# A long convolution done as two half-length transforms on a matmul array: 72 array fills in place of 96

## The chip, the core and the metric

The kernel runs on one core of a Trainium2 chip. A core has a matmul array (TensorE, PE in the profile), three engines for elementwise work (VectorE or DVE, ScalarE or ACT, GpSimd or POOL), a queue engine (SyncE or SP) that here issues nearly all transfers, and 16 DMA engines that carry them out. The metric is the time of one execution on the device in microseconds (us).

## What is computed

With S = 2048 positions and D = 512 channels:

```python
k_shift = sum(k_pad[:, t:t + S, :] * shift_k[:, ks - 1 - t] for t in range(4))   # 4 taps, causal
kv = k_shift * v
y = irfft(rfft(pad(kv)) * rfft(pad(ssm_k)))[:S]      # causal convolution of length S, one per channel
a = q * (y + kv * ssm_D)
b = relu(q @ w1) @ w2                                 # D -> 1792 -> D
g = sigmoid((q * gate_w).sum(-1))
out = g * a + (1 - g) * b
```

## The kernel before

**Two independent lines of work share the engines.** The one is the MLP b. Its inputs are split into a high and a low part, so that each product takes three matmuls of 128x512 (lines 310 to 312 for the first layer, 340 to 342 for the second). It runs in two eras of seven hidden blocks each, over four chunks of 512 positions. ACT writes the high part of the hidden block (`hh`, line 323), DVE the low part (`hl`, line 326); lines 257 and 260 split the loaded inputs and weights.

**The other is the convolution,** a transform of complex length 2048 in two steps, 64 times 32, such that the real part of the product's inverse is the causal convolution. It has three stages, with a round through DRAM between them:

- *First stage* (`stage1`, eight chunks, each of two of the 16 columns into which the positions of a partition are laid): DVE makes kv (lines 439 to 455), then for the filter (`s1h`) and for kv (`s1x`) the array applies a 64-point transform. One matmul takes 64 rows to 128 (real and imaginary part of 64 frequencies), so two of them, side by side on the array, fill it once. ACT copies each result to an `ev` tile and SP stores it in the DRAM tensor `sa` (line 395): 64 stores.
- *Middle stage* (`conv_mid`, eight sets g of 256 complex frequencies): SP loads four `r` tiles from `sa` (line 473, eight transfers a set) and the constants `cc`; the array does the 32-point transforms with 64x32 tiles, two fills for the filter (`f_h`) and two for kv (`f_x`, line 498); the filter's spectrum is copied to `ha` by DVE and ACT in turn (line 521); DVE makes the complex product, eight multiplications (line 533) and four sums (line 540) of 128x512 into `p`; the array applies the inverse 32-point transform in two fills of 32x64 tiles (`iv`, line 554); `bv` copies (lines 565 and 567) and four stores to `sb` (line 562) end the set. The inverse of set g-1 is issued in front of the transforms of set g.
- *End* (`conv_end`, four groups of four columns n): SP loads a `br` tile from `sb` for each n (line 599), the array applies the inverse 64-point transform, one fill each (`cy`, line 619), and DVE combines the result with q and the gate (lines 606 to 633) and with the MLP (line 580).

The second stage starts when all stores to `sa` have landed (`phase(2)`), the third when all stores to `sb` have (`phase(3)`). The four `r` tiles are as many as one set takes: the next set's loads wait until the fills of this set have read them.

**A planner writes the order of each engine's instructions** before the program is built (`Plan.order`). It plays the work through with a fixed cost for each operation and a room for each kind of buffer, and lets the convolution's fills go ahead of the MLP's matmuls as soon as their inputs are there by that reckoning. On the chip each engine then follows its list in order and waits where an input is late; this goes for SP too, whose transfers are issued one after another.

The transfers that matter here name their two sides in this way, the tile's side being 128 partitions of 512 values:

```python
nc.sync.dma_start(sa["hx".index(t), :, 16 * half + R * c + r], T["ev" + t, c, half, r])                                            # 395
nc.sync.dma_start(T[k("r", t, u)][:, i * D:(i + 1) * D], sa["hx".index(t), 4 * j:4 * j + 4].rearrange("k n d -> (k n) d"))      # 473
nc.sync.dma_start(sb[m:m + 4].rearrange("k n d -> (k n) d"), T[k("bv", j)])                                                      # 562
nc.sync.dma_start(rows(tile_of(k("br"), "br", 2 * D)), sb[:, n::16])                                                             # 599
```

Of the kernel before, what the change touches and what calls it, by code (L numbers as in the profile page):

```python
# [14 lines left out]
P = 128  # L15
# [25 lines left out]
def _constants():  # L41

    n1, k1 = np.arange(64)[:, None], np.arange(64)[None]
    w = _w((4 * k1 + 1) * 32 * n1)
    s1 = np.stack([w.real, w.imag], -1).reshape(64, 128)
    s1 = np.concatenate([s1, s1], 0)

    fw = np.zeros((2, 2, 32, NJ, 2, 32))  # L50
    iv = np.zeros((4, 32, 8, 2, 2, 2, 32))
    n2, k2 = np.arange(32)[:, None], np.arange(32)[None]
    for j in range(NJ):
        for b in range(2):
            k1 = 2 * j + b
            c = _w((4 * k1 + 1 + 256 * k2) * n2)
# [4 lines left out]
            c = np.conj(c.T)  # L61
            iv[j % 4, :, j // 4, 0, b, 0] = c.real
            iv[j % 4, :, j // 4, 1, b, 0] = -c.imag
            iv[j % 4, :, j // 4, 0, b, 1] = c.imag
            iv[j % 4, :, j // 4, 1, b, 1] = c.real
    cc = np.concatenate([fw.reshape(P, 8, 2 * P), iv.reshape(P, 8, 2 * P)], 2)


    c = np.conj(_w((4 * np.arange(64)[:, None] + 1) * 32 * np.arange(64)[None])) / S
    ib = np.stack([c.real, -c.imag], 1).reshape(P, 64)  # L70
    return s1, cc, ib
# [139 lines left out]
def build(tc, wf, xp, qn, kn, vn, hn, dn, sh, gw, w1, w2, cs1, ccc, cib, out):  # L211
# [13 lines left out]
    room = {"raw": RAW, "x": 4, "cv": 6, "m": 2, "hh": HB, "o": OB, "in": IN, "cc": 2, "acc": ACC, "tmp": TMP, "ev": EV, "r": RB,  # L225
# [150 lines left out]
    def stage1(c, rank, parts):  # L376

        ops = []
        deps = [s1ld] + [after for _, _, after, _ in parts]
        for t, key, after, give in parts:  # L380
            for r in range(R):
                def go(t=t, key=key, r=r):
                    z = slice(r * D, (r + 1) * D)
                    for half in range(2):
                        at = slice(64 * half, 64 * half + 64)
                        mm(bank(("s1" + t, c, half, r)), T["s1t",][at, :], T[key][at, z], start=True, stop=True)  # L386
# [12 lines left out]
        plan.chain(ops)  # L399
# [64 lines left out]
    def conv_load(g, gate):  # L464
# [12 lines left out]
        cc = add("SP", ISSUE, rank - 0.5, lambda: nc.sync.dma_start(tile_of(k("cc"), "cc", 4 * P), ccc[:, g]),  # L477
# [3 lines left out]
    def conv_mid(g, gate):  # L481
# [19 lines left out]
        last = list(ys.get(g - 1, {}).values())  # L501
# [10 lines left out]
        if g and IV_FIRST:  # L512
            put_iv(g - 1, ivp())
        fh = []
        ha = {}
        for o in range(2):
            f = link(TILES, lambda o=o: rounds("h", o), deps, ["cv"] * 2 + ["ha"] * 2, ["r"] * 2 if o else ())
            for b in range(2):
                cp = (nc.vector.tensor_copy if b == 0 else nc.scalar.copy)
                ha[o, b] = add("ACT" if b else "DVE", act_time(D, True) if b else dve_time(D), (0, rank),  # L520
                               lambda o=o, b=b, cp=cp: cp(tile_of(k("ha", o, b), "ha"), T[k("f", "h", o, b)]), [f], (), ["cv"], fifo=["ha"])
        if g and not IV_FIRST:
            put_iv(g - 1, ivp())
# [247 lines left out]
```

## Time and profile before

| what | value |
|---|---|
| median of 3 runs | 411.96 us (409.59 to 412.96) |
| the profiled execution | 410.51 us, of which 408.7 us are the span of the profile |
| busy: PE, DVE, ACT, POOL | 401.8, 274.2, 128.2, 1.4 us |
| PE clock granted | 0.999 of full speed |
| DMA | 90.94 MB, 222 GB/s over the span |

The span goes from the first instruction to the last. Busy times are those of single engines and overlap. A DMA share is the mean over the 16 DMA engines. In the tables of groups each row gives the line, the engine and the operation, the tile written and the tiles read, the count, the busy time and the mean duration of one; in the chain of work that ended last each row gives start, duration, engine, tile and line.

### The profile page before, as it was taken

To read this page: it belongs to the slowest core of one execution; us is meant where nothing else is said; L and a number is where in the kernel's file an instruction comes from. 1 tells how busy PE (TensorE), PEld (TensorE's weight loads), DVE (VectorE), ACT (ScalarE), POOL (GpSimd) and SP (SyncE) were. 2 spreads that over 40 slices of the span, in tenths; PEclk is the share of its full clock that TensorE was granted. 3 is DMA by queue.
4 is the path that set the end of the run, shared out by engine and by line. 5 is a ranking of instruction groups with operands and counts; after the bars stand their busy time and mean duration, and the time that the engine had idled before them with its cause. 6 is when DMAs were issued, how large, how long until landed. Compare 5 with 4: busy or idle time off the path is not lost.

```text
span 408.7 us, 6184 instructions
## 1 busy us (share of the span) xinstructions
PE 401.8 (98%) x2317; PEld 283.5 (69%) x2317; DVE 274.2 (67%) x420; ACT 128.2 (31%) x241; POOL 1.4 (0%) x6
## 2 busy tenths in 40 slices
PE   7999999999999999999999999999999999999996
PEld 6888667768667677667485857658478766765884
DVE  5699999745999302958785964968952577667511
ACT  6542552641554443421522320232411312002100
POOL 0000000000000000000000000000000000000000
PEclk9999999999999999999999999999999999999999
DMA  8986892994797784739684764837609684974011
GB/s 294 332 289 182 303 350 109 324 322 176 262 332 240 272 294 169 267 125 321 225 275 135 252 219 169 293 125 251 208 17 287 215 272 145 334 245 163 2 51 51
DMA packets 45487, 90.94 MB, mean 222 GB/s; under 512 B 4849, under 2 KB 5105, under 8 KB 45330
## 3 DMA queue, kind: packets, MB, share of 16 engines
q1 hardware_dynamic: 45394, 90.46, 64.8%
q8 instruction: 18, 0.29, 0.3%
q0 software_dynamic: 64, 0.10, 0.1%
q14 instruction: 11, 0.09, 0.1%
HBM read 61.18 MB, written 29.36 MB: 222 GB/s over the span
## 4 chain that ended last, share of the span: by engine, by line
PE 94%; DMA 3%; DVE 2%; ACT 0%; issue 0%; DVEq 0%; ACTq 0%
PE m L340 13%; PE m L341 12%; PE m L342 12%; PE m L310 11%; PE m L311 11%; PE m L312 11%; PE s1h L386 4%; PE f_h L498 4%; PE f_x L498 3%; PE s1x L386 3%; PE iv L554 3%; PE cy L619 3%; PE m L296 3%; DMA q<-qn 2%; DMA raw<-w 1%; DMA raw<-xp 1%
## 5 line engine op out<-in xcount | busy, mean ns | idle before, releaser
L340 PE MATMUL m<-w1h_h,hh 128*128 128x512 f32 x224 | 88.5, 395 | 0.0
L341 PE MATMUL m<-w1l_l,hh 128*128 128x512 f32 x224 | 87.4, 390 | 0.0
L342 PE MATMUL m<-w1h_h,hl 128*128 128x512 f32 x224 | 87.2, 389 | 0.0
L326 DVE SCALAR_TENSOR_TENSOR hl<-m,hh 128x512 fp32r<-128x512 f32 x56 | 38.3, 689 | 49.0 <-ACT hh L323 48.8
L323 ACT ACTIVATE hh<-m 128x512 fp32r<-128x512 f32 x56 | 33.3, 602 | 101.9 <-PE m L312 98.1
L310 PE MATMUL m<-xh_h,w0h_h 128*128 128x512 f32 x160 | 63.4, 396 | 0.4 <-DVE gs L611 0.4
L311 PE MATMUL m<-xl_l,w0h_h 128*128 128x512 f32 x160 | 62.4, 390 | 0.0
L312 PE MATMUL m<-xh_h,w0l_l 128*128 128x512 f32 x160 | 62.3, 389 | 0.0
L340 PEld LDWEIGHTS m<-w1h_h,hh 128*128 128x128 f32 x224 | 42.0, 188 | 17.3 <-issue 8.8
L342 PEld LDWEIGHTS m<-w1h_h,hl 128*128 128x128 f32 x224 | 42.0, 188 | 9.0
L341 PEld LDWEIGHTS m<-w1l_l,hh 128*128 128x128 f32 x224 | 42.1, 188 | 8.4
L310 PEld LDWEIGHTS m<-xh_h,w0h_h 128*128 128x128 f32 x160 | 30.0, 188 | 13.4 <-issue 5.7
L312 PEld LDWEIGHTS m<-xh_h,w0l_l 128*128 128x128 f32 x160 | 30.1, 188 | 6.4
L311 PEld LDWEIGHTS m<-xl_l,w0h_h 128*128 128x128 f32 x160 | 30.0, 188 | 5.9
L445 DVE TENSOR_TENSOR acc<-acc,tmp 128x1024 f32<-128x1024 f32 x24 | 29.3, 1223 | 0.6
L442 DVE TENSOR_TENSOR tmp<-in,sht_sht 128x512 f32<-128x512 f32 x32 | 21.3, 686 | 8.5 <-DMA in<-kn 8.3
L567 DVE COPY bv<-iv 128x512 f32<-128x512 f32 x16 | 10.3, 686 | 20.2 <-PE iv L554 20.2
L392 ACT COPY ev<-s1h 128x512 f32<-128x512 f32 x32 | 16.4, 599 | 19.7 <-PE s1h L386 17.7
L565 ACT COPY bv<-iv 128x512 f32<-128x512 f32 x16 | 8.6, 589 | 42.9 <-PE iv L554 36.0
L349 ACT COPY y<-m 128x512 f32<-128x512 f32 x16 | 9.4, 589 | 40.0 <-PE m L342 39.9
L533 DVE TENSOR_TENSOR p<-f_x,ha 128x512 f32<-128x512 f32 x32 | 19.9, 684 | 1.2 <-PE f_x L498 1.2
L533 DVE TENSOR_TENSOR ha<-f_x,ha 128x512 f32<-128x512 f32 x32 | 20.3, 681 | 0.0
(61 smaller groups left out, 449.4 us busy)
## 6 DMA issues: line engine op xcount, KB each, us to landing
sa<-ev SPq DMA_DIRECT2D x64, 256.0 KB, 4.2
r_h<-sa SPq DMA_DIRECT2D x32, 256.0 KB, 4.5
r_x<-sa SPq DMA_DIRECT2D x32, 256.0 KB, 5.2
sb<-bv SPq DMA_DIRECT2D x32, 256.0 KB, 3.6
br<-sb SPq DMA_DIRECT2D x16, 512.0 KB, 6.3
raw<-xp SPq DMA_DIRECT2D x28, 256.0 KB, 3.8
raw<-w SPq DMA_DIRECT2D x24, 256.0 KB, 4.3
in<-kn SPq DMA_DIRECT2D x10, 512.0 KB, 5.4
```

The lines of the kernel that those rows point to most:

```text
L310: mm(ps, part("h", f, k), T["x", "h", xe, c, k], start=k == 0, stop=False)
L311: mm(ps, part("h", f, k), T["x", "l", xe, c, k], start=False, stop=False)
L312: mm(ps, part("l", f, k), T["x", "h", xe, c, k], start=False, stop=k == 3)
L323: nc.scalar.activation(tile_of(("hh", era, c, f), "hh", dt=F32R, p=mp, bufs=HB), T["m1", era, c, f], AF.Relu)
L326: nc.vector.scalar_tensor_tensor(tile_of(("hl", era, c, f), "hl", dt=F32R, p=mp, bufs=HB), T["m1", era, c, f], 0.0, T["hh", era, c, f].bit ...
L340: mm(ps, T["hh", era, c, f][:, z], T["w", "h", 1, f], start=f == fs[0], stop=False)
L341: mm(ps, T["hh", era, c, f][:, z], T["w", "l", 1, f], start=False, stop=False)
L342: mm(ps, T["hl", era, c, f][:, z], T["w", "h", 1, f], start=False, stop=f == fs[-1])
L386: mm(bank(("s1" + t, c, half, r)), T["s1t",][at, :], T[key][at, z], start=True, stop=True)
L445: nc.vector.tensor_tensor(T["acc", c], T["acc", c], T[dst], op=OP.add)
L498: mm(ps[b][32 * j:32 * j + 32, :], T[k("cc")][at, 64 * j + 32 * o:64 * j + 32 * o + 32], T[k("r", t, j // 2)][at, (j % 2) * D:(j % 2 + 1) ...
L533: tt(src if o else tile_of(k("p", i, b), "p"), T[k("f", "x", o, b)], src, op=OP.mult)
```

## The change

The convolution is cut into halves of 1024 positions, filter and kv each. Both halves of both are transformed with complex length 1024 (32 times 32); the first half of the result is the product of the first halves, the second half comes from three products (first half by first half, turned by a quarter, and the two mixed ones), so three complex products take the place of one of twice the size.

- First stage: 32x64 tiles, eight to a fill, so one fill for each of filter and kv in a chunk where there were two. The two are no longer chained to one another. An `ev` tile now holds 64 rows for each of two positions.
- Middle stage: the fills are as many as before. The filter's spectrum goes into one `ha` tile of four planes, copied by ACT alone. DVE makes the products in five instructions, one over four planes and four over two, with the spectrum of kv read once per plane. GpSimd makes all sums, nine instructions over ten planes. The inverse of set g-2 (not g-1) is issued in front of set g.
- End: 64x32 tiles, one fill for two columns; a `br` tile holds two columns and is loaded by four transfers of 256 KB.
- `sa`, `sb` keep their shapes, with the 128 rows now (half, frequency, real or imaginary). The transfers to and from them take their DRAM side as 2 blocks of 64 rows. The rooms change with the tile sizes.

```diff
--- before.py
+++ after.py
-    n1, k1 = np.arange(64)[:, None], np.arange(64)[None]
-    w = _w((4 * k1 + 1) * 32 * n1)
-    s1 = np.stack([w.real, w.imag], -1).reshape(64, 128)
...
+    n1, k1 = np.arange(32)[:, None], np.arange(32)[None]
+    w = _w((4 * k1 + 1) * 64 * n1)
+    s1 = np.tile(np.stack([w.real, w.imag], -1).reshape(32, 64), (4, 1))
...
+    cc = np.concatenate([fw.reshape(P, 8, 2 * P), iv.reshape(P, 8, P)], 2)
...
+    ib = np.stack([c.real, -c.imag], 1).reshape(64, 32)
+    return s1, cc, np.tile(ib, (2, 1))
...
-    room = {"raw": RAW, "x": 4, "cv": 6, "m": 2, "hh": HB, "o": OB, "in": IN, "cc": 2, "acc": ACC, "tmp": TMP, "ev": EV, "r": RB,
...
-        ops = []
-        deps = [s1ld] + [after for _, _, after, _ in parts]
         for t, key, after, give in parts:
-            for r in range(R):
-                def go(t=t, key=key, r=r):
-                    z = slice(r * D, (r + 1) * D)
-                    for half in range(2):
-                        at = slice(64 * half, 64 * half + 64)
-                        mm(bank(("s1" + t, c, half, r)), T["s1t",][at, :], T[key][at, z], start=True, stop=True)
-
-                m = add("PE", TILES, (0, rank), go, deps if not ops else [ops[-1]], ["cv"] * 2, give if r == R - 1 else (), tiles=True)
-                ops.append(m)
-                for half in range(2):
-                    def out_(t=t, r=r, half=half):
-                        nc.scalar.copy(tile_of(("ev" + t, c, half, r), "ev"), T["s1" + t, c, half, r])
-
-                    def put(t=t, r=r, half=half):
-                        nc.sync.dma_start(sa["hx".index(t), :, 16 * half + R * c + r], T["ev" + t, c, half, r])
-
-                    v = add("ACT", act_time(D, True), (0, *rank), out_, [m], ["ev"], ["cv"])
-                    stores.append(add("SP", ISSUE, (-5000, *rank), put, [v], (), ["ev"], dma=ROW))
-        plan.chain(ops)
+            def go(t=t, key=key):
+                for a in range(4):
+                    ps = bank(("s1" + t, c, a))
+                    at = slice(32 * a, 32 * a + 32)
+                    for r in range(R):
+                        mm(ps[64 * r:64 * r + 64, :], T["s1t",][at, :], T[key][at, r * D:(r + 1) * D], start=True, stop=True)
+
+            m = add("PE", TILES, (0, rank), go, [s1ld, after], ["cv"] * 4, give, tiles=True)
+            for a in range(4):
+                def out_(t=t, a=a):
+                    nc.scalar.copy(tile_of(("ev" + t, c, a), "ev"), T["s1" + t, c, a])
+
+                def put(t=t, a=a):
+                    n = 16 * (a // 2) + R * c
+                    nc.sync.dma_start(sa["hx".index(t), 64 * (a % 2):64 * (a % 2) + 64, n:n + R].rearrange("m r d -> r m d"), T["ev" + t, c, a])
+
+                v = add("ACT", act_time(D, True), (0, *rank), out_, [m], ["ev"], ["cv"])
+                stores.append(add("SP", ISSUE, (-5000, *rank), put, [v], (), ["ev"], dma=ROW))
...
-                    nc.sync.dma_start(T[k("r", t, u)][:, i * D:(i + 1) * D], sa["hx".index(t), 4 * j:4 * j + 4].rearrange("k n d -> (k n) d"))
+                    src = sa["hx".index(t)].rearrange("(b m) n d -> b m n d", b=2)[:, 2 * j:2 * j + 2]
+                    nc.sync.dma_start(T[k("r", t, u)][:, i * D:(i + 1) * D], src.rearrange("b m n d -> b (m n) d"))
...
-        cc = add("SP", ISSUE, rank - 0.5, lambda: nc.sync.dma_start(tile_of(k("cc"), "cc", 4 * P), ccc[:, g]),
...
-        last = list(ys.get(g - 1, {}).values())
+        old = g - BEHIND
+        last = ys.get(old, [])
         if g < NJ // 4:
             h, x, cc = conv_load(g, gate)
             deps = h + x + [cc] + last
         else:
             deps = last
-        ivp = lambda: link(2 * TILES, lambda: inverse(g - 1), deps, ["cv"] * 4, ["p"] * 4 + ["cc"])
-        if g == NJ // 4:
-            put_iv(g - 1, ivp())
+        if old >= 0:
+            put_iv(old, link(2 * TILES, lambda: inverse(old), deps, ["cv"] * 4, ["p", "cc"]))
+        if g >= NJ // 4:
             plan.chain(chain)
...
+        planes = lambda z, u, n=2: T[k(z)][:, u * D:(u + n) * D].rearrange("p (r d) -> p r d", d=D)
+        ha = []
         for o in range(2):
-            f = link(TILES, lambda o=o: rounds("h", o), deps, ["cv"] * 2 + ["ha"] * 2, ["r"] * 2 if o else ())
+            f = link(TILES, lambda o=o: rounds("h", o), deps, ["cv"] * 2 + ([] if o else ["ha"]), ["r"] * 2 if o else ())
             for b in range(2):
-                cp = (nc.vector.tensor_copy if b == 0 else nc.scalar.copy)
-                ha[o, b] = add("ACT" if b else "DVE", act_time(D, True) if b else dve_time(D), (0, rank),
-                               lambda o=o, b=b, cp=cp: cp(tile_of(k("ha", o, b), "ha"), T[k("f", "h", o, b)]), [f], (), ["cv"], fifo=["ha"])
-        if g and not IV_FIRST:
-            put_iv(g - 1, ivp())
-        d = dve_time(D)
-        prev, y = {}, {}
-        for o in range(2):
-            fx = link(TILES, lambda o=o: rounds("x", o), deps, ["cv"] * 2 + ([] if o else ["p"] * 4), ["r"] * 2 if o else ())
-            for b in range(2):
-                for i in range(2):
-
-                    def mul(o=o, b=b, i=i):
-                        src = T[k("ha", i ^ o, b)]
-                        tt(src if o else tile_of(k("p", i, b), "p"), T[k("f", "x", o, b)], src, op=OP.mult)
-
-                    prev[o, b, i] = add("DVE", d, rank, mul, [fx, ha[i ^ o, b], prev.get((0, b, 0)), prev.get((0, b, 1))] if o else [fx, ha[i, b]],
-                                        (), ["cv"] if i else (), fifo=() if o else ["p"])
-                if o:
-                    for i in range(2):
-                        def join(b=b, i=i):
-                            tt(T[k("p", i, b)], T[k("p", i, b)], T[k("ha", 1 - i, b)], op=OP.add if i else OP.subtract)
-
-                        y[i, b] = add("DVE", d, rank, join, [prev[0, b, i], prev[1, b, i], prev[1, b, 1]], (), ["ha"])
-        ys[g] = y
+                e = "DVE" if (o, b) in HD else "ACT"
+
+                def out_(o=o, b=b, e=e):
+                    if not o and not b:
+                        tile_of(k("ha"), "ha", 4 * D)
+                    (nc.scalar.copy if e == "ACT" else nc.vector.tensor_copy)(T[k("ha")][:, (2 * b + o) * D:(2 * b + o + 1) * D], T[k("f", "h", o, b)])
+
+                ha.append(add(e, act_time(D, True) if e == "ACT" else dve_time(D), (0, rank), out_, [f] + ha[:1], (), ["cv"]))
+        fx = [link(TILES, lambda o=o: rounds("x", o), deps, ["cv"] * 2 + ([] if o else ["p"]), ["r"] * 2 if o else ()) for o in range(2)]
+
+        def mul(o, b, dst, u, src, n, deps, take=(), give=(), w=None):
+            def go():
+                if w:
+                    tile_of(k(dst), w[0], w[1] * D)
+                tt(planes(dst, u, n), T[k("f", "x", o, b)][:, None, :].to_broadcast([P, n, D]), planes("ha", src, n), op=OP.mult)
+
+            return add("DVE", dve_time(n * D), rank, go, [fx[o], *deps], take, give)
+
+        def sums(dst, src, u, n, deps, sign=1, give=()):
+            def go():
+                nc.gpsimd.tensor_tensor(planes("p", dst, n), planes("p", dst, n), planes(src, u, n), op=OP.add if sign > 0 else OP.subtract)
+
+            return add("POOL", 0.11 + n * 1.14, rank, go, deps, (), give)
+
+        a = mul(0, 0, "p", 0, 0, 4, ha, give=["cv"], w=("p", 4))
+        b = mul(1, 0, "ha", 2, 2, 2, [a])
+        c = mul(1, 0, "qa", 0, 0, 2, [b], ["qa"], ["cv"], ("qa", 2))
+        d = mul(0, 1, "qb", 0, 0, 2, [c], ["qb"], ["cv"], ("qb", 2))
+        e = mul(1, 1, "ha", 0, 0, 2, [d], give=["cv"])
+        z = sums(3, "ha", 2, 1, [b])
+        z = sums(2, "ha", 3, 1, [z], -1)
+        z = sums(1, "qa", 0, 1, [z, c])
+        z = sums(0, "qa", 1, 1, [z], -1, ["qa"])
+        z = sums(2, "qb", 0, 2, [z, d], 1, ["qb"])
+        z = sums(3, "p", 0, 1, [z])
+        z = sums(2, "p", 1, 1, [z], -1)
+        z = sums(3, "ha", 0, 1, [z, e])
+        z = sums(2, "ha", 1, 1, [z], -1, ["ha"])
+        ys[g] = [z]
         plan.chain(chain)
...
-                    c = 2 * P + P * o + 64 * b
-                    mm(ps[j][64 * b:64 * b + 64, :], T[k("cc")][at, c:c + 64], T[k("p", o, b)][at, :], start=o == 0, stop=o == 1)
+                    c = 2 * P + 64 * o
+                    z = (2 * b + o) * D
+                    mm(ps[j][64 * b:64 * b + 64, :], T[k("cc")][at, c:c + 64], T[k("p")][at, z:z + D], start=o == 0, stop=o == 1)
...
-                m = 4 * (4 * g + j)
-                nc.sync.dma_start(sb[m:m + 4].rearrange("k n d -> (k n) d"), T[k("bv", j)])
+                dst = sb.rearrange("(b k r) n d -> b k r n d", b=2, r=2)[:, 4 * g + j]
+                nc.sync.dma_start(dst.rearrange("b r n d -> b (r n) d"), T[k("bv", j)])
...
-            def ld(k=k, n=n):
-                nc.sync.dma_start(rows(tile_of(k("br"), "br", 2 * D)), sb[:, n::16])
-
+            if n % 2 == 0:
+                def ld(n=n):
+                    tile_of(("br", n), "br", 4 * D)
+                    for z in range(4):
+                        i, b = divmod(z, 2)
+                        src = sb[64 * b:64 * b + 64, 16 * i + n:16 * i + n + 2]
+                        nc.sync.dma_start(T["br", n][:, z * D:(z + 1) * D], src.rearrange("p n d -> n p d"))
+
+                e = add("SP", 4 * ISSUE, rank[1], ld, [gate], ["br"], dma=4 * ROW, fifo=["br"])
...
-        for n in ns:
-            def go(n=n):
-                ps = bank(("cy", n))
-                for i in range(2):
-                    mm(ps[64 * i:64 * i + 64, :], T["ibt",], T["br", n][:, i * D:(i + 1) * D], start=True, stop=True)
-
-            deps = [ibload] + [r[0] for r in ready.values()] + [r[1] for r in ready.values()]
-            m = add("PE", TILES, (0, 700.0 + ns[0]), go, [chain[-1]] if chain else deps, ["cv"], ["br"], tiles=True)
-            chain.append(m)
-            after(n, m, ready[n][1])
+        deps = [ibload] + [r[0] for r in ready.values()]
+        for m in range(2):
+            def go(two=ns[2 * m:2 * m + 2]):
+                for n in two:
+                    bank(("cy", n))
+
+                for to in range(4):
+                    for n in two:
+                        at = slice(64 * (n % 2), 64 * (n % 2) + 64)
+                        mm(T["cy", n][32 * to:32 * to + 32, :], T["ibt",][at, :], T["br", two[0]][at, to * D:(to + 1) * D], start=True, stop=True)
+
+            chain.append(add("PE", TILES, (0, 700.0 + ns[0]), go, deps if not chain else chain[-1:], ["cv"] * 2, ["br"], tiles=True))
...
-    for g in range(NJ // 4 + 1):
+    for g in range(NJ // 4 + BEHIND):
...
+BEHIND = 2
+HD = ()
...
-WB = 8
+WB = 7
...
-HAB = 4
-PB = 4
-BVB = 4
-BRB = 5
+HAB = 2
+PB = 2
+BVB = 3
+BRB = 3
```

More of the change, by code (lines that the diff above doesn't have):

```diff
@@ L60, in _constants @@
             fw[b, 1, :, j, 1] = c.real
[L61 to L71, printed above, removed]
+        c = np.conj(c.T)
+        iv[j % 4, :, j // 4, 0, 0] = c.real
+        iv[j % 4, :, j // 4, 1, 0] = -c.imag
+        iv[j % 4, :, j // 4, 0, 1] = c.imag
+        iv[j % 4, :, j // 4, 1, 1] = c.real
+    cc = np.concatenate([fw.reshape(P, 8, 2 * P), iv.reshape(P, 8, P)], 2)
+    c = np.conj(_w((4 * np.arange(32)[:, None] + 1) * 64 * np.arange(32)[None])) / (S // 2)
+    ib = np.stack([c.real, -c.imag], 1).reshape(64, 32)
+    return s1, cc, np.tile(ib, (2, 1))
 def _flat(r):
@@ L223, in build @@
     sb = dram.tile([P, 32, D], F32, name="sb")
-    room = {"raw": RAW, "x": 4, "cv": 6, "m": 2, "hh": HB, "o": OB, "in": IN, "cc": 2, "acc": ACC, "tmp": TMP, "ev": EV, "r": RB,
+    room = {"raw": RAW, "x": 4, "cv": 6, "m": 2, "hh": HB, "o": OB, "in": IN, "cc": BEHIND + 1, "qa": 1, "qb": 1, "acc": ACC, "tmp": TMP, "ev": EV, "r": RB,
             "ha": HAB, "p": PB, "bv": BVB, "br": BRB, "t": TB, "q": QB, "w1": WB, "w2": WB}
@@ L578, in go @@
                 if z.start == 0:
-                    tile_of(("o", n), "o", p=mp)
+                    tile_of(("o", n), "o")
                 nc.vector.scalar_tensor_tensor(T["o", n][:, z], T[key][:, z], T["gs", n][:, 2:3], T["t", n][:, z], op0=OP.mult, op1=OP.add)
@@ L614, in conv_end @@
         chain = []
-        for n in ns:
-            def go(n=n):
-                ps = bank(("cy", n))
-                for i in range(2):
-                    mm(ps[64 * i:64 * i + 64, :], T["ibt",], T["br", n][:, i * D:(i + 1) * D], start=True, stop=True)
-            deps = [ibload] + [r[0] for r in ready.values()] + [r[1] for r in ready.values()]
-            m = add("PE", TILES, (0, 700.0 + ns[0]), go, [chain[-1]] if chain else deps, ["cv"], ["br"], tiles=True)
-            chain.append(m)
-            after(n, m, ready[n][1])
+        deps = [ibload] + [r[0] for r in ready.values()]
[8 more added lines that the diff above has]
+            chain.append(add("PE", TILES, (0, 700.0 + ns[0]), go, deps if not chain else chain[-1:], ["cv"] * 2, ["br"], tiles=True))
+            for n in ns[2 * m:2 * m + 2]:
+                after(n, chain[-1], ready[n][1])
         plan.chain(chain)
@@ L654, in build @@
         load_first(k, -1002.5 + k)
-    s1ld = add("POOL", 1.04, 0, lambda: nc.gpsimd.dma_start(tile_of(("s1t",), "s1c", P, p=wp), cs1), [w], dma=ROW // 4)
+    s1ld = add("POOL", 1.04, 0, lambda: nc.gpsimd.dma_start(tile_of(("s1t",), "s1c", 64, p=wp), cs1), [w], dma=ROW // 4)
     for f in ERAS[0][G:]:
@@ L682, in build @@
     p2 = add("SP", 0.0, -1e3, lambda: phase(2), stores)
-    for g in range(NJ // 4 + 1):
+    for g in range(NJ // 4 + BEHIND):
         conv_mid(g, p2)
     p3 = add("SP", 0.0, -1e3, lambda: phase(3), sbstores)
-    ibload = add("POOL", 1.04, 5, lambda: nc.gpsimd.dma_start(tile_of(("ibt",), "ibt", 64), cib), [p3], dma=ROW // 8)
+    ibload = add("POOL", 1.04, 5, lambda: nc.gpsimd.dma_start(tile_of(("ibt",), "ibt", 32), cib), [p3], dma=ROW // 8)
     order_n = [4 * c + s for c in CHUNKS[1] for s in range(4)]
```

12 lines of the change are left out of this document (3 added, 9 removed).

## The prediction

> **What bounds the kernel now.** I read the page first: the busy times, then the slices and the queues.
>
> ```profile
> span 408.7 us, 6184 instructions
> PE 401.8 (98%) x2317; PEld 283.5 (69%) x2317; DVE 274.2 (67%) x420; ACT 128.2 (31%) x241; POOL 1.4 (0%) x6
> DMA packets 45487, 90.94 MB, mean 222 GB/s; under 512 B 4849, under 2 KB 5105, under 8 KB 45330
> q1 hardware_dynamic: 45394, 90.46, 64.8%
> q0 software_dynamic: 64, 0.10, 0.1%
> ```
>
> PE is busy for 98% of the span, so as it stands an array fill that goes is time that goes. DVE has a third of the span free. The DMA engines are used to 65%: all 16 together, and that word will matter. The profiled execution took 410.51 us, 1.8 us beside its span and 1.45 us under the median of 411.96; my sums are made against 410.51.
>
> The chain of work that ended last, in order of time, gives the prices on PE:
>
> ```profile
> 40.91 1.92 PE s1h L386 x8
> 42.83 1.72 PE s1x L386 x8
> 253.49 1.90 PE iv L554 x32
> 255.39 1.92 PE f_h L498 x32
> 257.31 1.72 PE f_x L498 x32
> 259.02 0.43 PE m L340
> 259.68 0.24 PE m L342
> 270.13 1.90 PE iv L554 x32
> 374.66 3.58 PE cy L619 x16
> ```
>
> Each of these pieces is two fills (the last is four). Two fills cost 1.72 us when fills ran before them and 1.92 when the MLP did, so a fill is 0.86 us and going over to fills 0.20; the way back costs 0.43 - 0.24 = 0.19. One set of the middle stage follows the next after 270.13 - 253.49 = 16.64 us.
>
> The list of transfers is the view that decides this case. I quote the groups that the change touches, the first and the last row among them; there are 302 issues in all, `dn` one of them.
>
> ```profile
> sa<-ev SPq DMA_DIRECT2D x64, 256.0 KB, 4.2
> r_h<-sa SPq DMA_DIRECT2D x32, 256.0 KB, 4.5
> r_x<-sa SPq DMA_DIRECT2D x32, 256.0 KB, 5.2
> sb<-bv SPq DMA_DIRECT2D x32, 256.0 KB, 3.6
> br<-sb SPq DMA_DIRECT2D x16, 512.0 KB, 6.3
> ...
> out<-o SPq DMA_DIRECT2D x15, 256.0 KB, 3.6
> ...
> s1c_s1t<-cs POOLq DMA_DIRECT2D x1, 64.0 KB, 3.4
> ibt_ibt<-cib POOLq DMA_DIRECT2D x1, 32.0 KB, 2.5
> tmp_dt<-dn SPq DMA_DIRECT2D x1, 2.0 KB
> ```
>
> Now count the small packets. No transfer of data moves rows under 512 bytes on q1, so the 4849 packets under 512 B are what a transfer leaves when it is complete. Take 16 for each of the 301 SP transfers that have 128 rows on both sides, 32 for the two of POOL (half of q0's 64) and **one** for `dn`, which has a single row: 4816 + 32 + 1 = 4849, to the packet. So a transfer is dealt out by its slowest dimension, a share with its own completion to each DMA engine that takes part: 128 rows go to 16 engines, one row to one.
>
> **What the change does to the transfers.** Before, the DRAM side of every transfer to and from `sa` and `sb` could be written as 128 rows at one distance. After, it is 2 blocks of 64 rows, blocks and rows at different distances (`m r d -> r m d` with two r; `b (m n) d`, `b (r n) d` with two b; `p n d -> n p d` with two n). The slowest dimension is then 2 on that side and 128 on the tile's. By the count above I take the number of engines to be what both sides can be dealt to: two. The number of transfers is 64 stores to `sa`, 64 loads of `r`, 32 stores to `sb` and 32 loads of `br` (eight tiles of four): 192 of 256 KB, 50.3 of the kernel's 90.46 MB. Nothing in the diff gives one of them other engines than the next, so I take the same two for all; that they rotate is a rival.
>
> The Trainium skill, "DMA: Bandwidth & Descriptors", section "Why a DMA increments its semaphore by 16 and not by 1", states this as a rule: the number of engines is the largest up to 16 that divides the slowest dimension of both sides, and on the hardware queues they are the lowest-numbered ones. By that rule the sum is the one that follows; that `dn` left one packet and the others 16 agrees with it, and no run here shows a dimension of 2.
>
> The price of an engine's work comes from the table of stretches (length and busy times first, the last two columns DMA share and GB/s):
>
> ```profile
> 0.00:40.00 40.00, 37.86 (x166) 31.64 (x167) 31.34 (x45) 19.23 (x32) 0.87 (x5) 1.00 0.81 278
> 163.00:305.00 142.00, 141.38 (x1187) 91.55 (x1186) 106.43 (x172) 40.11 (x73) 0.00 (x0) 1.00 0.61 206
> 305.00:327.00 22.00, 22.00 (x99) 17.75 (x99) 8.82 (x23) 5.91 (x13) 0.53 (x1) 1.00 0.73 240
> 397.00:400.00 3.00, 3.00 (x15) 2.49 (x14) 0.00 (x0) 0.00 (x0) 0.00 (x0) 1.00 0.23 87
> ```
>
> In the last one a single 256 KB store runs alone: 87 GB/s at a share of 0.23 of 16 engines is 23.6 GB/s for one engine. In the crowded stretch 305 to 327 it is 240 / (0.73 x 16) = 20.5. With two engines at work the memory is not crowded, so I take 23.6 and keep 20.5 for the range. One of the 192 transfers then holds each of the two engines for 131,072 B / 23.6 GB/s = 5.55 us (6.39).
>
> - The 192: 192 x 5.55 = 1066 us (1227).
> - These two engines' sixteenth of the other 40.1 MB: 2.51 MB, 106 us (122), of which 278 GB/s x 40 us / 16 = 0.70 MB, 29 us (34), is done by 40 us.
> - What lies ahead: the first fill of stage one is at 40.91, so 40 us.
> - Where the two engines must stand still: in each set of the middle stage the next loads wait for the fills and the stores for the inverse, since the four `r` tiles hold one set. From the last load's last byte to the next transfer's first: 1.90 us (`iv`), 0.69 (a `bv` copy) and some 2.9 us to land and to issue (the lone store lands after 3.6 us, of which 0.69 is transfer), 5.5 us, times 8 = 44. The two gates between stages: 5 us each, 10.
> - Behind the last `cy`: 408.7 - 374.66 = 34 us, as before.
>
> 40 + 1066 + 106 - 29 + 44 + 10 + 34 = 1271 us (1443). SP is one queue and its transfers are carried out in their order, so the MLP's loads stand behind these; PE, in its own fixed order, may have to do a stretch of MLP (259.02 to 270.13, 11.1 us) after a late load before it reaches the next set, with the two engines idle meanwhile: nothing to 8 x 11.1 = 89 us. I take the middle, 45. With 1.8 us around the span: **1318 us**, between 1271 and 1534; the lower end is opened to 1230, as the end stage's last loads may cover some of the 34 us.
>
> In the first stage there is no such standstill: seven `ev` tiles are 39 us of stores in the queue, more than PE and DVE need for the next chunk.
>
> **What the change does elsewhere** (all of it lies beside those transfers, if they are as I say):
>
> ```profile
> L533 DVE TENSOR_TENSOR p<-f_x,ha 128x512 f32<-128x512 f32 x32 | 19.9, 684 | 1.2 <-PE f_x L498 1.2
> L540 DVE TENSOR_TENSOR p<-p,ha 128x512 f32<-128x512 f32 x32 | 20.2, 683 | 0.0
> L521 DVE COPY ha<-f_h 128x512 f32<-128x512 f32 x16 | 11.0, 687 | 0.7 <-PE f_h L498 0.4
> L521 ACT COPY ha<-f_h 128x512 f32<-128x512 f32 x16 | 9.4, 588 | 2.7 <-PE f_h L498 2.7
> L567 DVE COPY bv<-iv 128x512 f32<-128x512 f32 x16 | 10.3, 686 | 20.2 <-PE iv L554 20.2
> L439 DVE TENSOR_TENSOR acc<-in,sht_sht 128x1024 f32<-128x1024 f32 x8 | 9.8, 1222 | 5.0 <-PE s1x L386 5.0
> ```
>
> - *PE*: 16 fills fewer in the first stage, 8 in the end: 24 x 0.86 = 20.6 us. Against it, filter and kv are no longer chained, and there is one inverse more by itself: at most 8 + 1 more goings to and fro at 0.39, 3.5 us. 17.1 us net.
> - *DVE*: a set had 14 operations of 0.684, 9.6 us. A second 512 columns in the same instruction cost 1222 - 684 = 538 ns, so four planes are 2.30 and the five instructions 2.30 + 4 x 1.222 = 7.2 us. 2.4 us less a set, on an engine that is not the bound: nothing.
> - *ACT*: two more copies a set, 1.18 us, on an engine busy 40 of 142 us there. All six banks turn over in a set, so PE may wait for the pair of copies, 1.18 against a fill of 0.86: nothing to 0.3 us a set, I take nothing.
> - *GpSimd*: the trace of before has no such sum. Below stands DVE's price, 0.683 + one double one, 6.7 us a set in nine instructions; above I know no row. The inverse comes two sets later, so a set's sums cost nothing until they need more than the 16.64 us between sets, 2.5 times DVE's price. I take no cost. The skill's "GPSIMD Engine Reference", section 3.1, has 4497 against 2293 ns for such an add, 1.96 times, by which a set would be an estimated 13 us and still free.
> - *Rooms*: fewer `br` and `bv` tiles and one weight less ahead: covered by the slack that PE's full row shows, 0.
>
> **The rivals.**
> - *The transfers spread over 16 engines all the same* (the dimension is counted otherwise than I read it from one transfer of one row). For it: only `dn` speaks of anything but 128. Then PE remains the bound, and the change gives what its fills say: 410.51 - 17.1 = **393 us, faster**. It decides from about 8 engines on: twelve transfers of a set, 3.15 MB in 16.64 us, are 189 GB/s, which 8 engines of 23.6 carry.
> - *Two engines each, but in rotation*: a load takes 5.55 + 2.9 = 8.4 us in place of 4.5 to 5.2, eight at once on eight pairs. Up to 4 us a set in which PE has MLP to do: 393 to 425, about 400.
> - *Spread over 16, and GpSimd becomes the pace*: at four times DVE's price a set's sums take 26.8 us, 10.2 more than a set; less the one set of lead, 8 x 10.2 - 16.6 = 65 us, 458 in place of 393.
>
> **How the numbers follow.** Two engines 0.72 (1318 us), spread over 16 at 393 us 0.20, rotation 0.04, GpSimd as the pace 0.04. The forecast's own range is 1230 to 1534 us and holds perhaps 0.62; for 8 in 10 the range must reach to the case of 393, so it goes from 390 to 1540, almost empty in its middle. One per cent, 4 us, is about what a measurement of this kernel tells from no change. Faster: 0.20 and half of the rotation, 0.22. Within 1%: 0.01. Slower: 0.77.
>
> **What would show it.** Packets under 512 B: with two engines 125 x 16 + 192 x 2 + 33 = 2417, with sixteen 317 x 16 + 33 = 5105. A DMA share near 2/16 with the moved part at some 47 GB/s for most of the span; `sa`, `r`, `sb` and `br` landing after tens of us where they took 3.6 to 6.3; PE with long waits in front of `s1`, `f_h` and `cy`, ended by transfers; POOL far from busy. If PE is near 98% and the stores land in 4 to 5 us, the step that failed is the dealing out by the slowest dimension; if the packets are 2417 and the time is a third of mine, the two engines aren't the same ones throughout; if it is a tenth off, it is the rate of one engine or the standstills.

## The result, and the profile after

The changed kernel takes 1139.0 us (median of four, 1137.28 to 1139.97) against 410.88 us: 2.77 times as long (95% interval 2.756 to 2.784). The page of the changed kernel, its busy times, the last two rows of its slices (40 slices of 28 us) and its queues:

```profile
span 1138.1 us, 6600 instructions
PE 569.0 (50%) x2509; PEld 316.8 (28%) x2509; DVE 265.4 (23%) x348; ACT 137.3 (12%) x257; POOL 102.1 (9%) x78
...
DMA  6521131241131112111122121111112112113321
GB/s 230 187 101 51 69 132 52 75 141 51 67 132 67 51 58 94 59 66 57 51 83 81 51 89 51 58 51 57 52 51 84 51 55 83 59 52 121 115 84 57
DMA packets 43058, 90.40 MB, mean 79 GB/s; under 512 B 2417, under 2 KB 3713, under 8 KB 42898
...
q1 hardware_dynamic: 42962, 89.93, 22.0%
```

Nothing that computes is near full. PE's busy time has risen from 401.8 to 569.0 us although it has fewer fills: its granted clock was 0.694 over the span (0.999 before), so its matmuls took longer. It stands idle for half of the span all the same, and the chain below runs through the transfers. The small packets are 2417, the number that two completions for each of the 192 transfers give. And the bandwidth has a floor: many slices stand at 51 or 52 GB/s, where before single slices reached 350. Two stretches of the changed kernel (last columns: PE clock granted, DMA share, GB/s), the second while PE does the filter's pair of fills:

```profile
260.00:300.00 40.00, 17.58 (x49) 9.21 (x47) 8.35 (x9) 5.69 (x10) 0.00 (x0) 0.61 0.13 52
644.00:648.00 4.00, 3.62 (x20) 0.59 (x20) 0.00 (x0) 0.00 (x0) 0.00 (x0) 0.52 0.13 51
```

A share of 0.13 of 16 is two engines; 51 GB/s over two is 25.5 each. The transfers to and from `sa`, as SP issued them (least, median and greatest time of the issue, first and last start):

```profile
L388 SPq DMA_DIRECT2D sa<-ev x64: 487/4949/5819, 22.0 to 390.6; - x64
L466 SPq DMA_DIRECT2D r_h<-sa x32: 487/4994/5551, 400.8 to 814.6; - x32
L466 SPq DMA_DIRECT2D r_x<-sa x32: 507/4999/5592, 416.8 to 840.5; - x32
```

The issue itself takes 5 us, where its median was 0.43 (`sa`) before: once the two engines' queues are full, SP stands at each transfer for about the time that one takes to go through. The chain of work that ended last, two of the middle stage's rounds (start, duration):

```profile
625.77 18.37 DMA r_h<-sa
644.18 3.67 PE f_h L491 x20
647.86 3.10 SPq L466
651.00 19.39 DMA r_x<-sa
670.43 3.62 PE f_x L491 x20
```

Four loads, fills, four loads, fills: PE does the fills of the filter as soon as the filter's loads are there, while those of kv are still on their way.

### The profile page after: what moved, and what is told of

Same layout as the page of the kernel before. It is cut to its first block, busy times and chain, and to the rows that moved or that the text cites. A ratio compares the mean times of both kernels' runs of the same rounds, so it can differ in the third digit from the quotient of the medians.

```text
span 1138.1 us, 6600 instructions
## 1 busy us (share of the span) xinstructions
PE 569.0 (50%) x2509; PEld 316.8 (28%) x2509; DVE 265.4 (23%) x348; ACT 137.3 (12%) x257; POOL 102.1 (9%) x78
## 2 busy tenths in 40 slices
DMA packets 43058, 90.40 MB, mean 79 GB/s; under 512 B 2417, under 2 KB 3713, under 8 KB 42898
## 4 chain that ended last, share of the span: by engine, by line
DMA 43%; SPq 26%; PE 16%; issue 2%; DVE 1%; ACT 1%; DVEq 0%; ACTq 0%
DMA sa<-ev 11%; SPq L611 10%; DMA r_x<-sa 10%; DMA sb<-bv 9%; SPq L466 7%; DMA r_h<-sa 7%; SPq L388 4%; DMA in<-kn 3%; PE m L335 2%; PE m L305 2%; PE f_x L491 2%; PE m L336 2%; PE m L337 2%; PE m L306 2%; SPq L614 2%
## 5 line engine op out<-in xcount | busy, mean ns | idle before, releaser
L335 PE MATMUL m<-w1h_h,hh 128*128 128x512 f32 x224 | 97.4, 435 | 74.5 <-DVE hl L321 42.2
L305 PE MATMUL m<-xh_h,w0h_h 128*128 128x512 f32 x160 | 74.2, 464 | 113.3 <-DVE hl L321 81.6
L491 PE MATMUL f_x<-r_x,cc 64*32 64x512 f32 x256 | 63.9, 992 | 113.4 <-DMA r_x<-sa 71.8
L531 POOL TENSOR_TENSOR p<-p,ha 128x512 f32<-128x512 f32 x32 | 41.2, 1310 | 776.5 <-DVE ha L525 742.1
L491 PE MATMUL f_h<-r_h,cc 64*32 64x512 f32 x256 | 58.2, 939 | 104.0 <-DMA r_h<-sa 104.0
L525 DVE TENSOR_TENSOR p<-f_x,ha 128x2048 f32<-128x2048 f32 x8 | 18.3, 2290 | 266.8 <-PE f_x L491 266.8
L306 PE MATMUL m<-xl_l,w0h_h 128*128 128x512 f32 x160 | 70.6, 441 | 0.0
L636 PE MATMUL cy<-br,ibt_ibt 64*32 64x512 f32 x128 | 33.9, 785 | 49.5 <-DMA br<-sb 49.5
L305 PE MATMUL m<-xh_h,w0h_h_g 128*128 128x512 f32 x48 | 23.2, 483 | 67.4 <-DVE hl L321 40.3
L491 PEld LDWEIGHTS f_x<-r_x,cc 64*32 64x32 f32 x256 | 8.8, 136 | 167.6 <-DMA r_x<-sa 90.9
```

The costliest lines, as they stand in the source:

```text
L305: mm(ps, part("h", f, k), T["x", "h", xe, c, k], start=k == 0, stop=False)
L306: mm(ps, part("h", f, k), T["x", "l", xe, c, k], start=False, stop=False)
L335: mm(ps, T["hh", era, c, f][:, z], T["w", "h", 1, f], start=f == fs[0], stop=False)
L491: mm(ps[b][32 * j:32 * j + 32, :], T[k("cc")][at, 64 * j + 32 * o:64 * j + 32 * o + 32], T[k("r", t, j // 2)][at, (j % 2) * D:(j % 2 + 1) ...
L531: nc.gpsimd.tensor_tensor(planes("p", dst, n), planes("p", dst, n), planes(src, u, n), op=OP.add if sign > 0 else OP.subtract)
```

## The experiments

Two theories stood against each other. *Mine*: the loss is the time of two DMA engines, and nothing else in the change costs much. *The rival*: the wide products and GpSimd's sums hold the middle stage, or the spread of the transfers isn't by the slowest dimension.

### All transfers on 16 engines: rows128

The edit, cut to the addresses and the order of the constants' rows:

```diff
-    sa = dram.tile([2, P, 32, D], F32, name="sa")
-    sb = dram.tile([P, 32, D], F32, name="sb")
+    sa = dram.tile([2, 2, 32, 64, D], F32, name="sa")
+    sb = dram.tile([2, 32, 64, D], F32, name="sb")
...
+ sa["hx".index(t), a % 2, n:n + R].rearrange("r m d -> (r m) d")            # store: 128 rows
+ sa["hx".index(t), :, :, 2 * j:2 * j + 2].rearrange("b n m d -> (b n) m d") # load: 64 pairs of rows
+ sb[:, :, 2 * k:2 * k + 2].rearrange("b n r d -> (b n) r d")                # store, k = 4 * g + j
+ sb[b, 16 * i + n:16 * i + n + 2].rearrange("n p d -> (n p) d")             # load
...
+ fw.transpose(0, 2, 1, 3, 4, 5), iv.swapaxes(4, 5)                          # the constants' rows to match
```

> The changed kernel with the same work on every engine, but sa laid out as (half, column, row) and sb likewise, and the rows inside a stationary tile reordered to match, so that the DRAM side of each of the 192 transfers has 64 or 128 rows as its slowest dimension. Theory (the two-engine transfers are the whole of the loss): 5105 small packets, transfers landing in 4 to 6 us, issues under 0.6 us, PE above 95% busy, 393 us, within 388 to 405. Rival (GpSimd's sums, at 1310 ns an add in the changed kernel, or the wide products hold the middle stage): small packets 5105 all the same, but PE waits in front of iv or f_x and the time stays above 420 us.

406.28 us, 0.9874 of before (0.9832 to 0.9915). Its page:

```profile
span 403.0 us, 6600 instructions
PE 390.1 (97%) x2509; PEld 274.4 (68%) x2509; DVE 270.4 (67%) x348; ACT 135.6 (34%) x257; POOL 105.0 (26%) x78
...
DMA packets 45746, 90.41 MB, mean 224 GB/s; under 512 B 5105, under 2 KB 6401, under 8 KB 45586
...
q1 hardware_dynamic: 45650, 89.94, 64.8%
```

The same computation in the same order on PE, 733 us less: the whole loss was the way in which the transfers were laid out. This edit also moves the rows to other places in DRAM; that it is the dealing out which counts, and not where the rows lie, is shown by blocks2 against blocks32 and by split64 below, which keeps the layout of the change. But 406 is 13 us above the 393 that was expected, a little outside the expected span: against 411.89 us for the kernel before in the same round, only 5.6 of the 17.1 us that the fills promised were saved. The other 12 are taken up below.

### How many engines, in the kernel before: blocks2, blocks4, blocks8, blocks32

Here only the 64 stores to `sa` of the kernel *before* change, by spare rows that cut their 128 rows into blocks:

```diff
-    sa = dram.tile([2, P, 32, D], F32, name="sa")
+    NB = 2                                     # 4, 8, 32
+    sa = dram.tile([2, NB, P // NB + 1, 32, D], F32, name="sa")
...
-    sa["hx".index(t), :, 16 * half + R * c + r]
+    sa["hx".index(t), :, :P // NB, 16 * half + R * c + r]
...
+    # the loads address block 4 * j // (P // NB), still 128 rows in one piece
```

> The kernel before with one edit: sa has a spare row after each 64, so that the 64 stores to it have 2 blocks of 64 rows on the DRAM side; the loads keep their 128 rows. Theory (slowest dimension 2 means two engines of about 25 GB/s, the same two each time): the first stage moves 8.4 MB plus a sixteenth of 11.7 MB through each of them, 9.1 MB, 365 us in place of 106, so 410 + 259 = 670 us (630 to 710); small packets 237 x 16 + 64 x 2 + 33 = 3953; stores take 5 us to issue once the queue is full. Rival (two engines in rotation, or the loss in the changed kernel comes from its other parts): under 430 us.

> As blocks2, with 4 blocks of 32 rows. Theory (the number of engines is what divides the slowest dimension of both sides): four engines, 4.2 + 0.73 MB through each in the first stage, 197 us in place of 106, so about 500 us (470 to 530); small packets 237 x 16 + 64 x 4 + 33 = 4081. Rival (anything but 128 rows falls to two engines): as blocks2.

> As blocks2, with 8 blocks of 16 rows. Theory: eight engines, 2.1 + 0.73 MB through each, 113 us in place of 106, so 410 to 425 us; small packets 237 x 16 + 64 x 8 + 33 = 4337. This is the point from which the prediction said that PE stays the bound. Rival (a spare row or the split itself costs): above 440 us.

> The kernel before with a spare row after each 4 of sa, so that the stores have 32 blocks of 4 rows. Theory: 16 engines as before, small packets 4849, within 1% of 411 us; the spare rows cost nothing, so the loss of blocks2 and blocks4 is the number of blocks. Rival (blocks as such cost time): above 420 us.

| blocks | expected us | measured us | small packets, expected and counted |
|---|---|---|---|
| 2 | 670 | 663.42 | 3953 |
| 4 | about 500 | 505.17 | 4081 |
| 8 | 410 to 425 | 429.34 | 4337 |
| 32 | 411 within 1% | 412.14 | 4849 |

Each of the four was run once, as were sa128 and split64 below. The kernel before stood at 411.89 us beside the first three (seven runs from 410.51 to 413.30) and at 412.08 beside the last. The packets came out to the unit in all four. The page of the kernel with two blocks, and the row of its stores:

```profile
span 661.6 us, 6184 instructions
...
DMA packets 44591, 90.94 MB, mean 137 GB/s; under 512 B 3953, under 2 KB 4209, under 8 KB 44434
```

```profile
L396 SPq DMA_DIRECT2D sa<-ev x64: 489/4950/5870, 44.0 to 391.6; - x64
```

So one edit to the layout of `sa`, with as many bytes and instructions as before, costs 250 us. The number of engines is the largest up to 16 that divides the slowest dimension of both sides, as the Trainium skill has it ("DMA: Bandwidth & Descriptors", section "Why a DMA increments its semaphore by 16 and not by 1"); the runs agree for 2, 4, 8 and 32. By the counts, each store left 2, 4, 8 and 16 small packets. Spare rows as such cost nothing (32 blocks). Eight blocks came out 4 us above the expected span and 17 us above the kernel before. ACT waited 30.0 us for stores to free `ev` tiles, against 0.2 before, so eight engines aren't yet enough there; each store also took 0.60 us to issue in place of 0.43. Which of the two costs how much wasn't tested.

### Does it add up: sa128

> The changed kernel with only sa laid out anew: the 64 stores to it and the 64 loads from it have 128 and 64 rows as their slowest dimension, the 64 transfers of sb and br keep their 2 blocks. Theory (the loss is the two engines' time, transfer by transfer): first stage as in rows128; from the first inverse at about 181 us eight sets of 4 x 5.0 us of stores and about 7 us of the two engines' share of the rest, 27 us each, to 397; then 166 us for the loads of br and 48 us behind them as in the changed kernel: about 610 us (570 to 640); small packets 253 x 16 + 64 x 2 + 33 = 4209. Rival (one of the stages has a loss of its own): outside 570 to 640 us.

612.09 us, with the edit of rows128 for `sa` alone:

```profile
span 610.3 us, 6600 instructions
...
DMA  8877797967743525262342311112211132313311
GB/s 304 314 262 293 274 312 264 320 245 245 243 155 111 174 85 187 95 198 97 137 143 82 112 50 51 67 42 81 81 65 52 52 140 94 111 52 111 111 59 53
```

The first stage is back at 240 to 320 GB/s, and from the first inverse on the two engines rule again. The first inverse started at 181.2 us and the first load of `br` at 397.0, as expected, and the whole came out 2 us from the sum. So neither the first nor the middle stage shows a loss of its own. For the end this is no test: its 166 + 48 us had been read from the changed kernel, where the same transfers run on two engines.

### The short way: split64

Each transfer as two of 64 rows, nothing else (one of the four places):

```diff
-    nc.sync.dma_start(dst.rearrange("b r n d -> b (r n) d"), T[k("bv", j)])
+    for b in range(2):
+        nc.sync.dma_start(dst[b].rearrange("r n d -> (r n) d"), T[k("bv", j)][64 * b:64 * b + 64, :])
...
```

> The changed kernel with each of the 192 transfers issued as two of 64 rows, in unchanged order and with the layouts of the change. Theory: 64 rows go to 16 engines too, small packets 125 x 16 + 384 x 16 + 33 = 8177; SP issues 192 transfers more, some 0.44 us each, 84 us, 12 more in a set of 16.6 us, beside other work: 405 to 425 us. Rival (blocks of 64 rows stay on few engines): above 700 us.

433.21 us with the 8177 small packets expected: cured of the two engines, but 27 us behind rows128 and slower than before, 8 us beyond the expected span. The queue row of its page:

```profile
DMA packets 48820, 90.44 MB, mean 210 GB/s; under 512 B 8177, under 2 KB 9473, under 8 KB 48658
...
q1 hardware_dynamic: 48722, 89.95, 70.6%
```

70.6% of 431.5 us is 305 us for each engine, 64.8% of 403.0 in rows128 is 261: the same bytes held the engines 17% longer, and SP issued 192 transfers more at 0.59 us. Which of the two cost the 27 us was not separated.

### Where 12 of the 17 us went: nosums, replan, poolsplit

In rows128 PE stood still for 12.9 us of the span, against 6.9 before, and was busy for 390.1 us, where 401.8 less the 17.1 is 384.7. Three waits in the middle stage are new (what waited, for what; us in total, times, longest):

```profile
PE f_h L491 <- DVE bv L574: 3.0, 1, 3.0
PE f_x L491 <- DVE bv L574: 1.9, 1, 1.9
PE m L305 <- DVE hl L321: 1.9, 1, 1.9
```

The one of `f_x`, at 287 us, is a `bv` copy that itself waited 3.87 us for a store to `sb`. The other two lie behind DVE's line 255. The chain of work at the first of them in time, that of `m`:

```profile
197.14 1.04 DVE w1l_l L255
198.18 0.39 issue
198.57 2.87 DVE w1l_l L255
201.44 0.61 DVE hl L321
202.10 0.50 PE m L305
202.59 0.38 PE m L306
202.97 0.43 PE m L307
203.40 0.43 PE m L305
```

One of DVE's subtractions (high part from the loaded tile, both in SBUF) takes 2.87 us. GpSimd's row at that time:

```profile
198.05 2.84 POOL L531 TENSOR_TENSOR p<-p,qb 128x1024 f32<-128x1024 f32 x1
```

The subtraction started at 198.57 us, while this sum ran, and ended 0.55 us after the sum did. The wait of `f_h` is of the same kind: the `bv` copy for which it waited stood on DVE behind four subtractions of `xl_l` that took 6.85 us together. All of line 255's subtractions of `xl_l` and `w1l_l` in that kernel, by tile (least, median, greatest ns), and then those of `xl_l` in the kernel before:

```profile
L255 DVE TENSOR_TENSOR xl_l<-raw,xh_h x28: 678/688/1816, 4.2 to 336.7; 128x512 fp32r<-128x512 f32 x28
L255 DVE TENSOR_TENSOR w1l_l<-raw,w1h_h x14: 671/690/2868, 15.2 to 202.0; 128x512 fp32r<-128x512 f32 x14
```

```profile
L260 DVE TENSOR_TENSOR xl_l<-raw,xh_h x28: 679/684/693, 4.1 to 339.9; 128x512 fp32r<-128x512 f32 x28
```

They are long only in the stretch in which GpSimd adds: ahead of 155 us line 255 took 22.22 us for 34 of them and behind 312 us 2.49 for 4, 0.65 and 0.62 each. GpSimd's rows and DVE's products in rows128, grouped by shape:

```profile
L531 POOL TENSOR_TENSOR p<-p,ha 128x512 f32<-128x512 f32 x32 | 42.3, 1343 | 198.8 <-DVE ha L525 198.8
...
L531 POOL TENSOR_TENSOR p<-p,qb 128x1024 f32<-128x1024 f32 x8 | 19.6, 2451 | 0.1
L525 DVE TENSOR_TENSOR ha<-f_x,ha 128x1024 f32<-128x1024 f32 x16 | 19.5, 1220 | 0.6
L525 DVE TENSOR_TENSOR p<-f_x,ha 128x2048 f32<-128x2048 f32 x8 | 18.3, 2290 | 19.0 <-ACT ha L516 15.3 <-PE f_x L491 3.7
```

The products, with one input in PSUM and one in SBUF, keep their 1.22 and 2.29 us beside GpSimd. This is what the Trainium skill says in "SBUF — State Buffer", section "Who interferes with whom": a DVE instruction with two SBUF inputs and a GpSimd instruction that reads SBUF share a read interface, and one of them waits for the other. Three kernels test what it costs; the edits are cut to the changed instruction or cost. Nosums leaves GpSimd's sums out, and its output lacks the terms that they add.

```diff
# nosums
-                nc.gpsimd.tensor_tensor(planes("p", dst, n), planes("p", dst, n), planes(src, u, n), op=...)
+                pass
# replan
-        return a, add("DVE", dve_time(D), rank, l, [a], (), give)
+        return a, add("DVE", 1.3 if LATE else dve_time(D), rank, l, [a], (), give)   # LATE: tiles of the second era
# poolsplit
-            nc.vector.tensor_tensor(tile_of(lo, ...), T[key], T[hi].bitcast(F32), op=OP.subtract)
+            (nc.gpsimd if LATE else nc.vector).tensor_tensor(tile_of(lo, ...), T[key], T[hi].bitcast(F32), op=OP.subtract)
```

> rows128 (the changed kernel with 64 or 128 rows as the slowest dimension of all its transfers) with GpSimd's nine sums of each set left out, each engine's order otherwise unchanged; the convolution is then without the cross terms. Theory (rows128 lost some 10 of the 17 us that its fills save because DVE's subtractions of two SBUF tiles, line 255, wait for GpSimd's sums: 18 of them in the middle stage took 22.7 us in place of 13.8 for 21 before): line 255 back at 0.69 us throughout, no PE wait behind it, 394 to 399 us. Rival (the loss comes from the unchained fills, the three bv tiles or ACT's four copies): line 255 back at 0.69 us, but 402 to 407 us.

> rows128 with one cost of the planner changed: 1.3 us in place of 0.65 for the 26 subtractions of line 255 that belong to the second era, as they took on the chip. Nothing is taken off any engine. Theory (the waits cost PE time because the written order does not know of them): PE's waits go, 396 to 402 us. Rival (DVE itself is short of time in the middle stage): within 1% of rows128, 402 to 410 us.

> rows128 with the 26 subtractions of the second era moved from DVE to GpSimd (planned at 1.25 us each), so that DVE has no instruction with two SBUF inputs beside GpSimd's work. Theory (the two engines hold each other up): the remaining operations of DVE keep their times, no PE wait behind line 255, 394 to 400 us, faster than both kernels. Rival (GpSimd becomes the pace: 104 + 26 x 1.31 = 138 us of some 157): sums late, PE waits in front of iv, 402 to 412 us.

| kernel | us | to before (95% interval) |
|---|---|---|
| rows128 | 406.28 | 0.9874 (0.9832 to 0.9915) |
| nosums | 396.01 | 0.9615 (0.9577 to 0.9654) |
| replan | 401.09 | 0.9747 (0.9718 to 0.9776) |
| poolsplit | 396.82 | 0.9682 (0.9619 to 0.9746) |

The subtractions of line 255 in the stretch of the middle stage, first in rows128, then in nosums (after the length: DVE's busy time in them and their count):

```profile
155.00:312.00 157.00, 22.72 (x18) 0.98 0.55 183
```

```profile
155.00:312.00 157.00, 13.15 (x21) 1.00 0.58 194
```

1.26 us each with the sums, 0.63 without them, and 10 us of time gone with them. Nosums alone doesn't tell the conflict from sums that come too late for the inverse; poolsplit, which keeps the sums and ends the conflict, gives the same 10 us within 1. Nosums in turn leaves DVE all its work, so what poolsplit gained isn't the relief of DVE. So the conflict is the cause, and for the unchained fills, the fuller ACT and the smaller rooms together only some 2 us of the 17.1 are left. Replan takes half of the 10 us back by order alone; it still has 3.8 us in which PE waits behind `bv` copies. Poolsplit puts both sides of the conflict on one engine:

```profile
span 394.2 us, 6611 instructions
PE 385.7 (98%) x2509; PEld 272.5 (69%) x2509; DVE 245.3 (62%) x322; ACT 135.6 (34%) x257; POOL 134.1 (34%) x104
```

At 396.82 us it is faster than both kernels, 3.2% under the one before. GpSimd, now with 134 us, did not become the pace. In the middle stage of its chain one long wait for a transfer is left, 4.38 us for a store of `bv` near 277 us, which points at the three `bv` tiles; a fourth wasn't tried.

## Why the prediction was right, and where it was not

The span was 1138.1 us against 1316 forecast (1139.0 against 1318 in time). The mechanism was right, the size was 178 us, 16%, too high. The time lies under the forecast's own range of 1230 to 1534 us. Only the wide one of 390 to 1540 holds it, in the part that was called almost empty; that one had been opened for the rival at 393 us, so that it holds the result says nothing for the sum. By the prediction's own terms:

| term | forecast us | measured us | from |
|---|---|---|---|
| ahead of the first moved transfer | 40 | 22 | first issue of `sa` |
| 192 transfers on two engines | 1066 | 987 | 131,072 B at 25.5 GB/s, 5.14 us each |
| their share of the rest, less what was done before | 77 | 82 | 2.48 MB at 25.5, less 288 GB/s over 22 us |
| standstills, gates, MLP behind late loads | 99 | 18 | what remains |
| behind the last `cy` | 34 | 29 | 1109 to 1138 |

Two terms make 160 of the 178 us: the rate of one engine (79) and the standstills (81). The 18 us are what remains, so they take up the small errors of the other rows too.

- *Dealt out by the slowest dimension, two engines*: right; packets 2417 forecast and counted. *The same two each time*: right; with pairs in rotation the floor would not be 51 GB/s.
- *The rate of one engine*: taken from a lone store as 23.6 GB/s, it was 25.5. A lone store has a beginning and an end in which the engine isn't full, while the two engines had the next transfer in their queue nearly all the time; that may be the reason, but no run separates it.
- *40 us ahead*: taken from the order before. The change unchained the filter's fill from kv's, and the planner moved the first one ahead; the prediction saw the unchaining and did not follow it here.
- *5.5 us of standstill a set, 44 us*: this step failed. It had PE start a set only when all eight loads were there, as the planner reckons; on the chip each matmul waits for its own tile. The filter's fills free two tiles while kv's loads still run. And SP's list holds stores of `bv` and loads for the MLP between one set's loads and the next: from 602 to 700 us its issues followed each other almost without a gap, so the two engines had work all the time, 51 GB/s straight through the fills at 644 us. For the same reason the MLP's stretch from 674 to 687 us, for which the prediction had added 45 us in all, did not stop them: they moved 51 GB/s or more throughout.
- *It decides from about 8 engines on*: reckoned for a set of the middle stage, and tested only on the first stage. There eight engines were not enough: with the 64 stores to `sa` in eight blocks the kernel before lost 17 us.
- *The rival at 393 us*: its price for the fills was sound, 15 of 17.1 us came back in nosums. Its "no cost" for the sums was wrong, but not in the way of the rival that named GpSimd as the pace: in rows128 the nine sums kept GpSimd busy 12.9 us a set, well inside 16.64, and still they cost 10 us, through DVE's subtractions, which the prediction did not weigh at all.
- *DVE*: four planes 2.30 forecast, 2.29 measured; right. *Rooms at nothing*: `bv` copies waited 3.87 us (rows128) and 4.38 us (poolsplit) for a store, and PE stood still 1.9 us behind the first, so the rooms cost a little.
- A slip beside the argument: the list of transfers has 304 issues, of which 302 are SP's; the count of the packets uses both numbers rightly.

## What to carry to other kernels

Read each transfer's two address patterns for their slowest dimension before anything else: a rearrangement that leaves 2 there gives away 14 of 16 DMA engines, and the small packets on the profile's page show it at once. Choose the DRAM layout so that this dimension is a multiple of 16 (here 32, 64 and 128 did), reordering a matmul's constants if need be, rather than splitting the transfer. And count GpSimd's work beside DVE not by GpSimd's time but by which DVE instructions read two SBUF tiles meanwhile; putting those on GpSimd as well gave 9.5 us here. Moving them to another time wasn't tried.

## What the runs showed of the hardware that was not expected

- An issue from SP took 5.0 us (median) while the two engines' queues were full, against 0.43 us before. The queue holds up whatever SP is to issue next: the load of `cc`, which 16 engines carry, took 4.92 us to issue at 395.66 us.
- The longest subtraction on DVE, 2.87 us, waited for the rest of the one sum that was running, of 1024 columns and 2.84 us, and ended 0.55 us behind it. GpSimd is held up as well: in rows128 two sums took 3.30 us where two undisturbed ones took 2.52.
- A wait of PE can cost more than its length. After it had stood still for 1.93 us at 200 us, the clock granted to it was 0.50 from 203 to 205 us and its matmuls came 0.43 us apart (the rows from 202.97 us above) in place of 0.23; from 206 us on it was 1.00 again. After the wait of 3.01 us at 227 us it was 0.50 from 230 to 233 us; after the one of 1.94 us at 287 us it stayed at 1.00.
